# Half differences issued one row half at a time, from two one-bank PSUM tiles

## The chip, the cores and the metric

The kernel runs on one core of a Trainium2 chip. A core has TensorE (PE in the profile; its weight loads are shown as PEld), VectorE (DVE), ScalarE (ACT), GpSimd (POOL) and SyncE (SP), which all take their instructions in order from a queue of their own, and 16 DMA engines. The metric is the time of one execution on the device in microseconds. TensorE writes to PSUM, 8 banks of 512 float32 values for each of 128 partitions; ScalarE and VectorE read it.

## What is computed

Two attentions over the same 2048 tokens, mixed by a gate for each token. Branch A is a sliding, dilated local attention (8 keys a query); branch B is a full attention of 32 heads that share one key and one value head.

```python
def _B_ref(x, wq, wk, wv, wo):
    B, S, D = x.shape
    H = 32; Dh = D // H
    q = (lambda x, *d: x.transpose(*d))((x @ wq).reshape(B, S, H, Dh), 0, 2, 1, 3)
    k = x @ wk
    v = x @ wv
    scores = jnp.einsum("bhqd,bkd->bhqk", q, k) * (Dh ** -0.5)
    p = _softmax(scores, axis=-1)
    o = jnp.einsum("bhqk,bkd->bhqd", p, v)
    return (lambda x, *d: x.transpose(*d))(o, 0, 2, 1, 3).reshape(B, S, H * Dh) @ wo
...
x = A_x
g = _sigmoid((x * gate_w).sum(-1, keepdims=True))
a = _A_ref(x, A_wqkv, A_wo)
b = _B_ref(x, B_wq, B_wk, B_wv, B_wo)
return g * a + (1 - g) * b
```

B = 1, S = 2048, D = 512, head size 16. The change is about the row maxima of branch B's scores, which the softmax subtracts.

## The kernel before

**Units.** Branch B is cut into 32 units: 4 blocks of 512 queries times 8 groups of 4 heads. A unit has 16 exponential steps, one for each block of 128 keys. In a step (exp_pair, weighted) two pairs of matmuls form the scores of 4 heads, keys on the partitions, ScalarE takes the exponential of each pair (2 banks), and four matmuls multiply the result with the values and add into the bank po. The maximum of each query's scores has to be known before its unit starts: it is written into two spare rows of the unit's query tile qst, so that the score matmul subtracts it.

**Maxima.** They come from a second set of score matmuls, queries on the partitions. A slot (v, pr, t, kc) is one unit, one pair of heads, one block of 128 queries and one block of 512 keys; it has two parts, odd = 0 and 1, which lie on the partitions 0 to 63 and 64 to 127 (two row halves of TensorE that can run side by side). The 2048 parts are settled in one of three ways:

- fill_pair: both parts of a slot into the two banks of m2 (pm in the profile), one VectorE reduction of 1024 values (L357).
- fill_one: one part into m1 (ps) or po, one reduction of 512 values (L368). In the exponential steps these are the "singles"; the function singles allows one in a step as long as more parts are left than two a remaining step, and 20 for each output row to come.
- half differences: for two slots with neighbouring key blocks, max(a, b) = (a + b)/2 + |a - b|/2. The keys' half sums and half differences stand in kcd (half_keys, half_parts). fill_diff multiplies the queries with the half differences into m2 (L422), and ScalarE writes the absolute values into a tile dd (L432); fill_sum multiplies with the half sums into m1 or po, and one fused VectorE operation adds |a - b|/2 and takes the maximum (L442), in place in dd. A group is two such slots: two difference matmuls, two absolute values, two sum matmuls, two fused operations, for four parts. In the projections dd is one tile; in an output phase it is two, taken in turn.

**Where half differences run.** In stream, which also issues the projections (queries, then 64 lumps of branch A's projection, 12 matmuls for each row half, 384 wide, two banks eb[0] or eb[1] in turn) and, in out_phase, the output rows (24 matmuls for each half and row, 512 wide). stream walks two positions, at[0] and at[1], one for each row half. In each step it gives each half its next matmul, or a single part in its stead (single, odd); only the other half advances then. After the step it may issue fill_diff, both halves at once, or fill_pair. A lump is emptied by two ScalarE copies (a_post, L251 and L252).

**Order.** All queues are written out in program order by a planner in the kernel: clk holds its clocks for PE, ACT and DVE, free the times at which banks come free, ready_d those of the absolute values; T_R, T_LAT, T_TTR and the like are its costs in microseconds, and after(engine, ready, duration) moves a clock on. pend holds the groups' parts that wait for their sum; slots are taken in order. fill_diff is called if no single part is open (half), pend is empty, and m2 is planned free within 0.1 us and VectorE within 1.3 us. fill_sum is called if its bank is at most 0.1 us and its absolute value at most 0.4 us from free. Output phases start at a unit's first step, when their units are done and the lead (parts settled, in units, less the unit reached) is below LEAD, 3.0; the last four output rows are spread over the last steps, when at most 9 parts are left (L1170).

The tiles m2, m1 and po come from one PSUM pool (pp). m2 serves as the bank of the last lump, of one pair of exponentials after an output phase (exp_pair with other), and of the last output rows too.

Of the kernel before, what the change touches and what calls it, by code (L numbers as in the profile page):

```python
# [6 lines left out]
F32 = mybir.dt.float32  # L7
# [6 lines left out]
P = 128  # L14
# [26 lines left out]
NH = NJ // 2  # L41
TO_END = 10
LEAD, M2S, M1S, E1S, PER_ROW = 3.0, 0.5, 0.3, 0.2, 20


T_R, T_LAT, T_EXP, T_RED2, T_RED1, T_W, T_TTR = 0.23, 0.20, 0.92, 1.14, 0.61, 1.21, 0.66


@with_exitstack
def gated_mix_kernel(ctx, tc, xt, wa, wk, wq, wo_a, wo_b, out):  # L50
# [24 lines left out]


    eb = [pp.tile([P, 2, 512], F32, name=f"pe{k}") for k in range(2)]
    m2 = pp.tile([P, 2, 512], F32, name="pm")
    m1 = pp.tile([P, 512], F32, name="ps")
    po = pp.tile([P, 512], F32, name="po")  # L80

    def split(hi, lo, src, eng=None):
        nc.scalar.activation(hi, src, AF.Copy)
# [266 lines left out]
        tasks.append((after("dve", 0, 0.34) + (2.0 if kcd and not pe else 0.1), shift_a, (v, mt)))  # L350

    def fill_pair(dst, key):
        v, pr, t, kc = slots.pop(0)
        m = unit_tile(v)
        for odd in range(2):
            max_mm(dst[:, odd, :], v, pr, t, kc, odd)
        nc.vector.tensor_reduce(m[:, :, pr, t, kc], dst, AX.X, ALU.max)  # L357
        free[key] = after("dve", after("pe", 0, T_R) + T_LAT, T_RED2) + 0.08
        filled(v, 2)
# [11 lines left out]


    sel, kcd, dd, pend, ready_d, formed, ended, wants = [], [], [], [], [0.0, 0.0], set(), set(), []
    hb = [(m2[:, 0, :], m2[:, 1, :]), (m1, po)]

    def half_sel():

# [10 lines left out]

    def half_keys(g):

        keys = ("m2", "m2") if g == 0 else ("m1", "po")
        clk["pe"] = max(clk["pe"], *(free[k] for k in keys))
        for x in range(2):
            for y in range(2):
                nc.tensor.matmul(hb[g][x], sel[0][:, x * y], kst[:, (2 * g + y) * 512:(2 * g + y + 1) * 512], start=(y == 0), stop=(y == 1))
        clk["pe"] += 1.2
        for k in keys:
            free[k] = clk["pe"] + 4.0
        tasks.append((clk["pe"] + 1.0, half_parts, (g, keys)))
# [20 lines left out]
    def half_mm(dst, v, pr, t, kc, x, odd):  # L420
        b = 64 * odd
        nc.tensor.matmul(dst, qst[home(v)[0]][b:b + 62, pr, t * P:(t + 1) * P], kcd[0][b:b + 62, kc // 2, x, :], start=True, stop=True)  # L422

    def fill_diff():
        v, pr, t, kc = slots.pop(0)
        slots.pop(0)
        for odd in range(2):
            half_mm(m2[:, odd, :], v, pr, t, kc, 1, odd)
        at = after("pe", 0, T_R) + T_LAT
        dd.append(dd.pop(0))  # L430
        for odd in range(2):
            nc.scalar.activation(dd[0][:, odd], m2[:, odd, :], AF.Abs)  # L432
            ready_d[odd] = after("act", at, 0.52) + 0.1
        free["m2"] = ready_d[1]
        pend.extend([(v, pr, t, kc, 0), (v, pr, t, kc, 1)])

    def fill_sum():
        v, pr, t, kc, odd = pend.pop(0)
        m = unit_tile(v)
        dst, key = ((m1, "m1"), (po, "po"))[odd]  # L440
        half_mm(dst, v, pr, t, kc, 0, odd)
        nc.vector.tensor_tensor_reduce(dd[0][:, odd], dst, dd[0][:, odd], 1.0, -FMAX, ALU.add, ALU.max, m[:, odd, pr, t, kc:kc + 1])  # L442
        free[key] = after("dve", max(clk["pe"] + T_R + T_LAT, ready_d[odd]), T_TTR) + 0.08
        filled(v, 2)

# [34 lines left out]
    pe, pexp, exped = [], {}, {}  # L480

    def exp_pair(s, pr, other=False, first=0):
        bank, key = (m2, "m2") if other else (eb[pr], f"e{pr}")
        u, kt = divmod(s, NJ)
        for odd in (first, 1 - first):
            b = 64 * odd
            nc.tensor.matmul(bank[:, odd, :], kst[b:b + 64, kt * P:(kt + 1) * P], qst[home(u)[0]][b:b + 64, pr, :], start=True, stop=True)  # L487
        e = px.tile([P, 2, 512], F32, name="pexp", bufs=6)
        nc.scalar.activation(e, bank, AF.Exp, scale=SCALE)  # L489
        free[key] = after("act", after("pe", free[key], T_R) + T_LAT, T_EXP)  # L490
        exped[s] = free[key]
        pexp[s, pr] = e
# [239 lines left out]
    def stream(seq, mm, done, pooled):  # L732

        at, told = [0, 0], 0
        ended.clear()
        while min(at) < len(seq):
            single, odd = None, -1
            if wants and all(free[k] <= clk["pe"] + 0.1 for k in (("m1", "po") if wants[0] else ("m2",))):
                half_keys(wants.pop(0))
            if pend:  # L740
                if free[("m1", "po")[pend[0][4]]] <= clk["pe"] + 0.1 and ready_d[pend[0][4]] <= clk["pe"] + 0.4:
                    single, odd = fill_sum, pend[0][4]
            elif paired() and not half or 1 in wants:
                pass
            elif fillable() and free["m1"] <= clk["pe"] + 0.1:
                single, odd = lambda: fill_one(m1, "m1"), half[0][4] if half else 0
            elif pooled and fillable() and free["po"] <= clk["pe"] + 0.1:
                single, odd = lambda: fill_one(po, "po"), half[0][4] if half else 0
            dur = 0.0
            for b in (0, 1) if odd != 1 else (1, 0):  # L750
                if b == odd:
                    now = clk["pe"]
                    single()
                    clk["pe"] = now
                elif at[b] < len(seq):
                    dur = mm(b, seq[at[b]])
                    at[b] += 1
            after("pe", 0, dur or T_R)
            if ended or 0 in wants:
                pass  # L760
            elif paired():
                if not half and not pend and max(free["m2"], clk["dve"] - 1.2) <= clk["pe"] + 0.1:
                    fill_diff()
            elif slots and fillable() and free["m2"] <= clk["pe"] + 0.1:
                clk["pe"] = max(clk["pe"], free["m2"])
                fill_pair(m2, "m2")
            while told < min(at):
                told += 1
                done(seq[told - 1])

    def out_phase(js, n, whole_unit):

        m = 3 * (C + n)
        items = {}

        def mm(b, at):
            x, j, i = at
            if j not in items:
                items[j] = out_items(j, n)
                clk["pe"] = max(clk["pe"], free[f"e{x % 2}"])  # L780
            st, mv = items[j][i]
            h = slice(64 * b, 64 * b + 64)
            nc.tensor.matmul(eb[x % 2][:, b, :], st()[h], mv[h], start=(i == 0), stop=(i == m - 1))  # L783
            return T_R

        def done(at):
            x, j, i = at
            if i % 4 == 3:
                run_tasks()
                run_pool()  # L790
            if x == len(js) - 1 and i == m - 5:
                ended.add(1)
            if x == 0 and i == 1:
                turn(j, 1)
            if x == 0 and i == 6:
                later.pop(j)()
            if i == 3 * n and j != js[-1]:
                prepare(js[x + 1], n)
            if i == m - 5 and j != js[-1]:
                turn(js[x + 1], 1 - x % 2)  # L800
            if i == m - 1:
                out_store(j, x % 2)
                if j != js[-1]:
                    later.pop(js[x + 1])()

        if whole_unit:
            formed.update((0, 1))
            free["po"] = max(free["po"], clk["dve"] + 0.1)
            dd[:] = [px.tile([P, 2, 512], F32, name="pexp", bufs=6) for _ in range(2)]
        stream([(x, j, i) for x, j in enumerate(js) for i in range(m)], mm, done, False)  # L810
        while pend:
            odd = pend[0][4]
            clk["pe"] = max(clk["pe"], free[("m1", "po")[odd]], ready_d[odd] - 0.3)
            fill_sum()
            clk["pe"] += T_R
        settle("sum", 0)
        formed.clear()
# [418 lines left out]
    for x in range(2):  # L1236
        for k, w in ((0, woh), (0, wol), (1, woh)):
            for t in range(2):
                nc.tensor.matmul(ends[2 * x + t], tls[x][:, k, t * P:(t + 1) * P], w[1][:, C - 1, :], start=(w is woh and k == 0 and x + t < 2), stop=(k == 1))
        for t in range(2):  # L1240
            j = NJ - 4 + 2 * x + t
            os = px.tile([P, D], F32, name="osl", tag="pexp", bufs=6)
            nc.vector.tensor_add(os, ends[2 * x + t], parts[j])
            (nc.sync, nc.scalar)[t].dma_start(out[0].rearrange("(p j) d -> p j d", j=NJ)[:, j, :], os)
    pe[0].release()
    p2[0].release()
    p2b[0].release()
# [26 lines left out]
```

## Time and profile before

| | us |
|---|---|
| median of 3 runs (1475.98 to 1476.28) | 1476.24 |
| the profiled execution | 1475.43 |
| its span | 1473.6 |
| first and last start of an absolute value in the projections | 101.9, 264.5 |
| the same in the output phases | 847.4, 1220.6 |

The times up to some 100 us are loads, keys, queries and first maxima; to some 266 us branch A's projections with half differences; then the exponential steps to the end, with output phases of 8 rows at about 846 us and of 4 rows at about 1186 us. A row of a group reads: line, engine, operation, output<-input, shapes and count | busy us, mean ns of one | idle time of the engine before it and what ended it. A row by stretch reads: start:end, length, busy us of each engine with its count of instructions, granted clock, DMA share, GB/s. A wait reads: who <- for whom: us in total, times, longest.

### The profile page before, as it was taken

How to read it: one execution, taken by the hardware profiler on the slowest of the kernel's cores; microseconds unless marked ns; L12 is line 12 of the kernel's file. 1: busy time of each engine (PE TensorE's matmuls, PEld its weight loads, DVE VectorE, ACT ScalarE, POOL GpSimd, SP SyncE). 2: the span in 40 equal slices, each digit the busy share in tenths (PEclk: the TensorE clock that was granted, in tenths of full speed). 3: DMA queues.
4: the chain of work that ended last, by engine and by line, in shares of the span. 5: the costliest groups of instructions: out<-in, count | busy, mean ns of one | idle time of the engine just before them, and what ended most of it. 6: DMA issues, size and time to landing. Idle time of an engine off the chain costs nothing.

```text
span 1473.6 us, 29548 instructions
## 1 busy us (share of the span) xinstructions
PE 1461.7 (99%) x10996; PEld 708.0 (48%) x10996; DVE 1193.9 (81%) x1855; ACT 1274.5 (86%) x1646; POOL 1032.6 (70%) x1828
## 2 busy tenths in 40 slices
PE   9999999999999999999999999999999999999998
PEld 5999889533333333333333376333333364333333
DVE  6976667789888888888898878899888878889712
ACT  5468988899999999999999978999999988999986
POOL 7876988887888979888889898888888330111220
PEclk9999999999999999999999999999999999999999
DMA  6754323121220211202112121120120000000110
GB/s 224 209 151 136 93 88 120 34 85 42 66 80 7 85 60 42 71 12 71 45 38 77 36 64 67 42 71 26 57 71 12 12 27 16 13 1 2 29 31 30
DMA packets 54080, 89.86 MB, mean 61 GB/s; under 512 B 18800, under 2 KB 35232, under 8 KB 49712
## 3 DMA queue, kind: packets, MB, share of 16 engines
q1 hardware_dynamic: 46928, 48.99, 11.4%
q0 software_dynamic: 6432, 37.94, 7.8%
q8 instruction: 86, 1.41, 0.4%
q10 hardware_dynamic: 576, 1.05, 0.2%
q14 instruction: 58, 0.48, 0.1%
HBM read 60.07 MB, written 27.35 MB: 59 GB/s over the span
## 4 chain that ended last, share of the span: by engine, by line
PE 91%; ACT 3%; POOL 3%; issue 1%; DVE 1%; DMA 1%; DVEq 0%; POOLq 0%; ACTq 0%
PE po L497 35%; PE pe L487 23%; PE pm L330 8%; PE ps L330 7%; PE pe L1098 7%; PE pe L783 4%; PE pm L422 2%; PE ps L422 1%; PE pm L851 1%; ACT dd L432 1%; PE po L422 1%; POOL qlo L222 1%; POOL qraw L215 1%; PE pe L185 1%; DMA xraw<-xt 1%
## 5 line engine op out<-in xcount | busy, mean ns | idle before, releaser
L489 ACT ACTIVATE pexp<-pe 128x1024 f32<-128x1024 f32 x1022 | 989.5, 1022 | 93.0 <-PE pe L487 90.8
L357 DVE TENSOR_REDUCE mx<-pm 128x2 f32<-128x1024 f32 x495 | 605.8, 1224 | 117.6 <-PE pm L330 113.8
L497 PE MATMUL po<-pexp,vst 128*32 128x512 f32 x4096 | 545.7, 605 | 0.0
L487 PE MATMUL pe<-qst,kst 64*128 64x512 f32 x1916 | 434.5, 447 | 0.4 <-ACT pexp L489 0.3
L487 PEld LDWEIGHTS pe<-qst,kst 64*128 64x128 f32 x1916 | 179.7, 183 | 473.7 <-ACT pexp L489 467.8
L368 DVE TENSOR_REDUCE mx<-ps 128x1 f32<-128x512 f32 x481 | 327.1, 680 | 3.7 <-PE ps L330 3.7
L330 PE MATMUL pm<-kst,qst 62*128 62x512 f32 x945 | 192.0, 396 | 0.3 <-DVE mx L357 0.3
L561 POOL TENSOR_TENSOR pr<-aext 128x256 f32<-128x256 f32 x256 | 182.5, 738 | 2.2 <-DMA aext<-ad 1.9
L330 PE MATMUL ps<-kst,qst 62*128 62x512 f32 x455 | 180.0, 396 | 0.2 <-DVE mx L442 0.2
L621 POOL TENSOR_TENSOR oa<-oa,av 128x256 f32<-128x256 f32 x224 | 164.1, 732 | 15.1
L497 PEld LDWEIGHTS po<-pexp,vst 128*32 128x32 f32 x4096 | 80.8, 108 | 178.2 <-issue 169.1
L618 POOL TENSOR_TENSOR av<-aext,lg 128x256 f32<-128x256 f32 x224 | 139.3, 622 | 12.7
L1098 PE MATMUL pe<-wah,xh 64*128 64x384 f32 (+1 forms) x504 | 109.8, 338 | 0.4 <-ACT gate L255 0.4
L1098 PE MATMUL pe<-wal,xh 64*128 64x384 f32 (+1 forms) x504 | 110.1, 337 | 0.0
L1098 PE MATMUL pe<-wah,xl 64*128 64x384 f32 (+1 forms) x504 | 109.9, 337 | 0.0
L432 ACT ACTIVATE dd<-pm 128x512 f32<-128x512 f32 x164 | 91.0, 608 | 17.8 <-PE pm L422 11.3
L442 DVE CUSTOM_DVE_ANT_0 dd<-ps,dd 128x512 f32<-128x512 f32 x82 | 56.7, 692 | 55.1 <-PE ps L422 28.9
L330 PEld LDWEIGHTS pm<-kst,qst 62*128 62x128 f32 x945 | 92.0, 187 | 2.8 <-DVE mx L357 1.0
L330 PEld LDWEIGHTS ps<-kst,qst 62*128 62x128 f32 x455 | 85.0, 187 | 5.5 <-DVE mx L368 1.7
L567 POOL TENSOR_TENSOR tr<-pr 128x512 f32<-128x512 f32 x64 | 81.7, 1277 | 4.1
L567 POOL TENSOR_TENSOR tr<-tr 128x256 f32<-128x256 f32 (+1 forms) x128 | 72.4, 566 | 8.3
L524 POOL TENSOR_TENSOR rl<-rl,gate_t 128x16 f32<-128x16 f32 x31 | 6.8, 220 | 100.4 <-DVE rl L518 99.9
(215 smaller groups left out, 1896.2 us busy)
## 6 DMA issues: line engine op xcount, KB each, us to landing
aext<-ad POOLq DMA_DIRECT2D x32, 1056.0 KB, 5.5
ad<-stage SPq DMA_DIRECT2D x32, 384.0 KB
qst<-qd SPq DMA_DIRECT2D x60, 128.0 KB
xraw<-xt SPq DMA_DIRECT2D x16, 256.0 KB
qd<-qhi SPq DMA_DIRECT2D x16, 256.0 KB
qd<-qlo SPq DMA_DIRECT2D x16, 256.0 KB
qst<-qd SPq DMA_DIRECT2D x60, 64.0 KB
qst<-ml SPq DMA_DIRECT2D x216, 2.0 KB
```

The source lines that it names most:

```text
L330: nc.tensor.matmul(dst, qst[home(v)[0]][b:b + 62, pr, t * P:(t + 1) * P], kst[b:b + 62, kc * 512:(kc + 1) * 512], start=True, stop=True)
L357: nc.vector.tensor_reduce(m[:, :, pr, t, kc], dst, AX.X, ALU.max)
L368: nc.vector.tensor_reduce(m[:, odd, pr, t, kc:kc + 1], dst, AX.X, ALU.max)
L432: nc.scalar.activation(dd[0][:, odd], m2[:, odd, :], AF.Abs)
L487: nc.tensor.matmul(bank[:, odd, :], kst[b:b + 64, kt * P:(kt + 1) * P], qst[home(u)[0]][b:b + 64, pr, :], start=True, stop=True)
L489: nc.scalar.activation(e, bank, AF.Exp, scale=SCALE)
L497: nc.tensor.matmul(po[32 * i:32 * i + 32, :], vst[:, kt, :], pexp[s, i // 2][:, i % 2, :], start=(kt == 0), stop=(kt == NJ - 1))
L561: nc.gpsimd.tensor_mul(pr[:, k], q, e[:, o:o + NH, AC:2 * AC])
L567: nc.gpsimd.tensor_add(nx, cur[:, :, 0:n], cur[:, :, n:2 * n])
L618: nc.gpsimd.tensor_mul(av, e[:, o:o + NH, 2 * AC:].rearrange("p j (h d) -> p j h d", d=DH), lg[:, w].unsqueeze(3).to_broadcast([P, NH, AG, ...
L621: nc.gpsimd.tensor_add(ao, ao, av)
L1098: nc.tensor.matmul(front[2 if x == last else x % 2][0][:, b, :n], l[h], r[h], start=(i == 0), stop=(i == 3 * C - 1))
```

## The change

A class Banks holds m2, either as one tile of two banks or as two tiles of one bank each; shape(n) releases the one form and takes the other. fill_pair, exp_pair with other, and the whole method ask for one tile; fill_diff and half_keys(0) ask for two. fill_diff now issues the difference matmul and the absolute value of one row half (odd), first 0, then 1; open_group holds the slot between the two. diff_half says whether one may go: no part of the same half in pend, its own bank planned free (half_free), VectorE's clock at most 1.6 us ahead. stream collects up to one part for each row half (lone) and issues these in place of that half's next matmul. pend carries the dd tile of its group. After the stream an open group is finished.

```diff
+M2H = 0.0
...
+class Banks:
...
+    def __init__(self, tc, name):
+        self.tc, self.name, self.pool, self.tiles = tc, name, None, ()
+        self.whole()
+
+    def shape(self, n):
+        if len(self.tiles) != n:
+            if self.pool:
+                self.pool.release()
+            self.pool = self.tc.alloc_tile_pool(name=self.name + "s", bufs=1, space=PSUM)
+            if n == 1:
+                self.tiles = [self.pool.tile([P, 2, 512], F32, name=self.name)]
+            else:
+                self.tiles = [self.pool.tile([P, 512], F32, name=self.name, tag=f"{self.name}{b}") for b in range(2)]
+        return self
+
+    def whole(self):
+        return self.shape(1).tiles[0]
+
+    def __getitem__(self, at):
+        if len(self.tiles) == 1:
+            return self.tiles[0][at]
+        return self.tiles[at[1]][:, at[2]]
...
-    m2 = pp.tile([P, 2, 512], F32, name="pm")
...
+    m2 = Banks(tc, "pm")
...
     def fill_pair(dst, key):
+        if dst is m2:
+            dst = m2.whole()
...
-    hb = [(m2[:, 0, :], m2[:, 1, :]), (m1, po)]
+    hb = {1: (m1, po)}
...
+        if g == 0:
+            hb[g] = (m2.shape(2)[:, 0, :], m2[:, 1, :])
...
+    open_group, half_free = [], [0.0, 0.0]
+
+    def diff_half():
+
+        if max(half_free) != free["m2"]:
+            half_free[:] = [free["m2"]] * 2
+        odd = len(open_group) and 1
+        if any(x[4] == odd for x in pend) or half_free[odd] > clk["pe"] - M2H or clk["dve"] - 1.6 > clk["pe"]:
+            return None
+        return odd
+
     def fill_diff():
-        v, pr, t, kc = slots.pop(0)
-        slots.pop(0)
-        for odd in range(2):
-            half_mm(m2[:, odd, :], v, pr, t, kc, 1, odd)
-        at = after("pe", 0, T_R) + T_LAT
-        dd.append(dd.pop(0))
-        for odd in range(2):
-            nc.scalar.activation(dd[0][:, odd], m2[:, odd, :], AF.Abs)
-            ready_d[odd] = after("act", at, 0.52) + 0.1
-        free["m2"] = ready_d[1]
-        pend.extend([(v, pr, t, kc, 0), (v, pr, t, kc, 1)])
+        if not open_group:
+            open_group.append(slots.pop(0))
+            slots.pop(0)
+            dd.append(dd.pop(0))
+            odd = 0
+        else:
+            odd = 1
+        v, pr, t, kc = open_group[0]
+        m2.shape(2)
+        half_mm(m2[:, odd, :], v, pr, t, kc, 1, odd)
+        nc.scalar.activation(dd[0][:, odd], m2[:, odd, :], AF.Abs)
+        half_free[odd] = ready_d[odd] = after("act", clk["pe"] + T_R + T_LAT, 0.54) + 0.1
+        free["m2"] = max(half_free)
+        pend.append((v, pr, t, kc, odd, dd[0]))
+        if odd:
+            open_group.clear()
 
     def fill_sum():
-        v, pr, t, kc, odd = pend.pop(0)
+        v, pr, t, kc, odd, d = pend.pop(0)
         m = unit_tile(v)
         dst, key = ((m1, "m1"), (po, "po"))[odd]
         half_mm(dst, v, pr, t, kc, 0, odd)
-        nc.vector.tensor_tensor_reduce(dd[0][:, odd], dst, dd[0][:, odd], 1.0, -FMAX, ALU.add, ALU.max, m[:, odd, pr, t, kc:kc + 1])
+        nc.vector.tensor_tensor_reduce(d[:, odd], dst, d[:, odd], 1.0, -FMAX, ALU.add, ALU.max, m[:, odd, pr, t, kc:kc + 1])
         free[key] = after("dve", max(clk["pe"] + T_R + T_LAT, ready_d[odd]), T_TTR) + 0.08
         filled(v, 2)
...
+        bank, key = (m2.whole(), "m2") if other else (eb[pr], f"e{pr}")
...
-            single, odd = None, -1
+            lone = {}
             if wants and all(free[k] <= clk["pe"] + 0.1 for k in (("m1", "po") if wants[0] else ("m2",))):
                 half_keys(wants.pop(0))
             if pend:
                 if free[("m1", "po")[pend[0][4]]] <= clk["pe"] + 0.1 and ready_d[pend[0][4]] <= clk["pe"] + 0.4:
-                    single, odd = fill_sum, pend[0][4]
-            elif paired() and not half or 1 in wants:
+                    lone[pend[0][4]] = fill_sum
+            elif open_group or paired() and not half or 1 in wants:
                 pass
             elif fillable() and free["m1"] <= clk["pe"] + 0.1:
-                single, odd = lambda: fill_one(m1, "m1"), half[0][4] if half else 0
+                lone[half[0][4] if half else 0] = lambda: fill_one(m1, "m1")
             elif pooled and fillable() and free["po"] <= clk["pe"] + 0.1:
-                single, odd = lambda: fill_one(po, "po"), half[0][4] if half else 0
+                lone[half[0][4] if half else 0] = lambda: fill_one(po, "po")
+            if open_group or paired() and not (ended or half or 0 in wants):
+                odd = diff_half()
+                if odd is not None and odd not in lone:
+                    lone[odd] = fill_diff
             dur = 0.0
-            for b in (0, 1) if odd != 1 else (1, 0):
-                if b == odd:
+            for b in sorted((0, 1), key=lambda b: b not in lone):
+                if b in lone:
                     now = clk["pe"]
-                    single()
+                    lone[b]()
                     clk["pe"] = now
                 elif at[b] < len(seq):
                     dur = mm(b, seq[at[b]])
                     at[b] += 1
             after("pe", 0, dur or T_R)
-            if ended or 0 in wants:
-                pass
-            elif paired():
-                if not half and not pend and max(free["m2"], clk["dve"] - 1.2) <= clk["pe"] + 0.1:
-                    fill_diff()
-            elif slots and fillable() and free["m2"] <= clk["pe"] + 0.1:
+            if not (ended or 0 in wants or open_group or paired()) and slots and fillable() and free["m2"] <= clk["pe"] + 0.1:
                 clk["pe"] = max(clk["pe"], free["m2"])
                 fill_pair(m2, "m2")
...
         stream([(x, j, i) for x, j in enumerate(js) for i in range(m)], mm, done, False)
+        if open_group:
+            clk["pe"] = max(clk["pe"], half_free[1], free["m2"])
+            fill_diff()
+            clk["pe"] += T_R
```

The other lines of the diff release the tiles at the end.

More of the change, by code (lines that the diff above doesn't have):

```diff
@@ L482, in exp_pair @@
     def exp_pair(s, pr, other=False, first=0):
-        bank, key = (m2, "m2") if other else (eb[pr], f"e{pr}")
+        bank, key = (m2.whole(), "m2") if other else (eb[pr], f"e{pr}")
         u, kt = divmod(s, NJ)
@@ L1244, in gated_mix_kernel @@
             (nc.sync, nc.scalar)[t].dma_start(out[0].rearrange("(p j) d -> p j d", j=NJ)[:, j, :], os)
+    m2.pool.release()
     pe[0].release()
```

## The prediction

> **What bounds the kernel now.** I read the page's busy times and chain first, then the costliest groups, then stretches of time one by one, because the kernel has stages with different limits.
>
> ```profile
> PE 1461.7 (99%) x10996; PEld 708.0 (48%) x10996; DVE 1193.9 (81%) x1855; ACT 1274.5 (86%) x1646; POOL 1032.6 (70%) x1828
> ...
> PE 91%; ACT 3%; POOL 3%; issue 1%; DVE 1%; DMA 1%; DVEq 0%; POOLq 0%; ACTq 0%
> ```
>
> TensorE is busy for 99% of the span and is 91% of the chain: the order on its queue, and what makes that queue wait, set the time. The change touches three stretches, those that hold half differences (L432 and L442). In the busy times by stretch they stand out by their weight loads:
>
> ```profile
> core 0: us, PE busy (x) PEld busy (x) DVE busy (x) ACT busy (x) POOL busy (x), PEclk, DMA share, GB/s
> 100.00:266.00 166.00, 164.87 (x1662) 150.77 (x1660) 110.84 (x343) 142.92 (x334) 136.75 (x224) 1.00 0.35 108
> 846.00:916.00 70.00, 68.80 (x601) 51.23 (x601) 56.77 (x164) 55.75 (x107) 63.54 (x102) 1.00 0.15 48
> 1186.00:1223.00 37.00, 36.22 (x314) 25.93 (x310) 29.60 (x84) 28.90 (x55) 13.52 (x19) 1.00 0.08 27
> ```
>
> Call them the projection stretch and the two output stretches (8 rows, then 4). The granted clock is 1.00 in all. ScalarE idles 23.1, 14.2 and 8.1 us in them, 45.4 us in all. The absolute values are counted by the group of L432, split by the same stretches:
>
> ```profile
> 100.00:266.00 166.00, 90.97 (x164) 1.00 0.35 108
> 846.00:916.00 70.00, 39.30 (x72) 1.00 0.15 48
> 1186.00:1223.00 37.00, 19.65 (x36) 1.00 0.08 27
> ```
>
> The same stretch's groups on ScalarE give the number of projections (a lump in the code) in it, 56:
>
> ```profile
> L251 ACT ACTIVATE stage<-pe 128x384 f32<-128x384 f32 x56 | 27.5, 492 | 5.2 <-PE pe L1098 3.0 <-POOL wal L84 0.8 <-PE po L422 0.4
> ```
>
> A group (one call of fill_diff before) has two of them, so there are 82, 36 and 18 groups, 136 in all; each settles four maxima of 512 scores, at 2 x 90.97/164 = 1.11 us of ScalarE.
>
> Between these stretches the exponential steps run. TensorE alone, two steps of them:
>
> ```profile
> 432.91 1.07 PE L497 MATMUL po<-pexp,vst 128*32 128x512 f32 x8
> ...
> 434.24 0.40 PE L330 MATMUL pm<-kst,qst 62*128 62x512 f32 x2
> 434.48 0.41 PE L487 MATMUL pe<-qst,kst 64*128 64x512 f32 x2
> 434.73 0.40 PE L330 MATMUL ps<-kst,qst 62*128 62x512 f32 x1
> 435.05 1.07 PE L497 MATMUL po<-pexp,vst 128*32 128x512 f32 x8
> ...
> 436.94 1.06 PE L497 MATMUL po<-pexp,vst 128*32 128x512 f32 x8
> ```
>
> A step with a pair of maxima (pm) and a single one (ps) takes 435.05 - 432.91 = 2.14 us; the next, with the pair alone, 1.89 us. So a single costs about 0.24 us. VectorE's reductions of singles, by stretch, say how many there are:
>
> ```profile
> 270.00:846.00 576.00, 177.87 (x262) 1.00 0.17 53
> 916.00:1186.00 270.00, 82.66 (x122) 1.00 0.14 46
> 1223.00:1389.00 166.00, 51.49 (x76) 1.00 0.03 9
> ```
>
> 460 of them, in nearly every step. A maximum that is settled in a stretch with half differences takes a single out of a step: the function singles drops them as soon as two per remaining step suffice. That is where a gain can come from.
>
> **What the change does.** It adds no operation: per group there are still four 512-wide matmuls, two absolute values, two fused sum-and-maximum operations. It moves the two difference matmuls. Before, both row halves are issued together, only when no sum is pending; after, each half goes alone beside the other half's projection matmul, as soon as its own bank is free in the plan, its own sum has been issued and VectorE is planned at most 1.6 us behind. So it changes how many groups the planner fits in, and what TensorE's queue waits for. Here is such a wait, in order of time:
>
> ```profile
> 182.53 0.34 PE L1098 MATMUL pe<-wal,xh 64*128 64x384 f32 x2
> ...
> 182.68 0.08 DVE L442 DVE_READ_ACCUMULATOR2_ANT mx<- 128x1 f32 x1
> ...
> 182.71 0.35 PE L1098 MATMUL pe<-wah,xl 64*128 64x384 f32 x2
> ...
> 182.86 1.15 ACT L432 ACTIVATE dd<-pm 128x512 f32<-128x512 f32 x2
> ...
> 183.59 0.69 DVE L442 CUSTOM_DVE_ANT_0 dd<-ps,dd 128x512 f32<-128x512 f32 x1 [0.22 <-ACT dd L432]
> ...
> 183.90 0.48 ACT L251 ACTIVATE stage<-pe 128x384 f32<-128x384 f32 x1
> 184.06 0.19 PEld L422 LDWEIGHTS pm<-kcd,qst 62*128 62x128 f32 x2 [0.41 <-ACT dd L432]
> 184.06 0.49 PE L422 MATMUL pm<-kcd,qst 62*128 62x512 f32 x2
> ...
> 184.21 0.08 DVE L442 DVE_READ_ACCUMULATOR2_ANT mx<- 128x1 f32 x1
> ...
> 184.27 0.50 ACT L252 ACTIVATE two<-pe 128x384 f32<-128x384 f32 x1
> ...
> 184.39 0.34 PE L1098 MATMUL pe<-wal,xh 64*128 64x384 f32 x2
> ```
>
> The pair of absolute values ends at 184.01; the next pair of differences starts at 184.06, both halves, though the first bank must have been read by about 183.5. One tile for two banks makes half 0 wait for half 1.
>
> *What a group costs TensorE.* Projection pairs follow each other in 182.71 - 182.53 = 0.18 us; in the step above the pair pm at 434.24 gives way to the next matmul at 434.48, 0.24 us. Four half matmuls are two such pairs: 0.46 us (0.23 each) by this stage's rate, before as after. What hides them: nothing, TensorE is the bound. A group is worth four singles at 0.24 us less: 0.96 - 0.46 = 0.50 us net.
>
> *How many groups more.* I stepped both issue rules by hand with the planner's constants (0.18 us a projection step, 0.23 + 0.20 to the absolute value, 0.54 for it, 0.66 for the fused operation, 0.8 for a projection's two copies). The old rule settles at a group per 1.49 us, ScalarE idling some 0.45 us of it, and with the copies at 1.61 groups per projection of 12 steps. The new one starts the next half 0 while half 1 is still read: after a first lump the planned ScalarE has hardly a gap, and three lumps of 2.88 us hold 11 absolute values, 1.83 groups per lump. 82 x 1.83/1.61 = 93; the gates and other small operations take their share from both, so I take 92, 10 more. In an output row (24 steps of 0.23, 2.4 us of copies on ScalarE) the plan holds 4.5 groups at 87% of ScalarE; at the 96% of the new rule 0.96 x (6.0 + 0.46g) = 2.4 + 1.08g gives 5.3. That is 6 and 3 more. Sum: 19. Bounds: 0 (the plan's ScalarE is full already) and 45.4/(1.11 - 0.46) = 70 (ScalarE never idle). I take 19, near the lower end, because the planner's clock counts, not the chip's, and its ScalarE is at 90% already.
>
> *What waits come and go.* Waits of the projection stretch, then of the first output stretch:
>
> ```profile
> DVE dd L442 <- ACT dd L432: 23.2, 27, 3.3
> ACT dd L432 <- PE pm L422: 11.3, 18, 0.9
> PEld pm L422 <- ACT dd L432: 11.3, 39, 0.7
> ...
> ACT dd L432 <- DVE mx L442: 5.9, 8, 0.9
> ```
>
> ```profile
> ACT pexp L432 <- PE pm L422: 12.2, 20, 1.2
> ...
> PEld pe L783 <- ACT turned L679: 4.1, 7, 0.7
> PEld pm L422 <- ACT pexp L432: 2.8, 12, 0.3
> ```
>
> TensorE's wait for the bank, 11.3 + 2.8 us of idle weight load (39 waits of 0.29 us, part of it under a running matmul), is what separate tiles can shorten: the least is 0, a gain of 14 us. Against that stands the buffer dd: the projection stretch has one. The absolute value overwrites what the fused operation of the group before has read (above, 182.68 + 0.08, then 0.10 us to the start at 182.86). From 182.86 over the fused operation at 183.59 and its read-out to 184.29 and 0.10 more is 1.53 us: a half cannot come round faster, while the new plan puts some groups 1.08 us apart. ScalarE then stands in that wait, with the projection's copies (L251, L252) queued behind it, and TensorE follows when its bank is late. By that loop a lump with 1.64 groups takes 1.53 x 1.64 + 0.45 (the two copies take 0.87 us, 183.90 to 184.77 above; 1.53 - 1.11 = 0.42 of it fits into the loop's gap) = 2.96 us against 12 x 0.18 + 0.46 x 1.64 = 2.91 of TensorE: 0.05 us x 56 lumps = 3 us. So the waits are put at +3 us, between -14 and the +14 of the rival below. The output stretches have two dd buffers and are spared this.
>
> The tiles that change shape cost only at a change of stage, where pm is drained before as after; I set them at 0, and at 4 such changes with one 0.41 us wait each it would be 2 us. More maxima done early raise the planner's lead, which can put an output stretch 16 steps later, past some of the loads of queries on SP's queue and of branch A's work on POOL: the same rows, copies and stores, at 0 as long as the last four rows still come after the singles.
>
> *A rule against it.* The Trainium skill (TensorEngine Tiling (Array Packing), Performance Considerations, on the PSUM bottleneck) says that splitting the array into tiles speeds up TensorE but not the emptying of PSUM. The stretch's ScalarE row agrees (142.92 of 166 us); by that rule no group comes on top, which is the second rival below.
>
> **The sum.** 19 groups x 4 x 0.24 = 18.2 us off the steps; 19 x 0.46 = 8.7 on in the stretches; +3 waits: -6.5 us. The profiled execution took 1475.43 us (span 1473.6), so 1468.9; the median of the runs lies 0.8 higher, which gives **1470 us**.
>
> **Rivals.**
>
> *The gaps of ScalarE really fill.* If the earlier issue fills ScalarE two thirds of the way to its bound, 45 groups at 0.50 us: -22 us, 1454. For it: the 12.2 us in which ScalarE waited for pm. Against: the planner issues by its own clock, and that one is nearly full.
>
> *Nothing changes.* ScalarE sets the number of groups, a few come on top and their 0.46 us and the waits eat them: 1473 to 1478. For it: 86% of ScalarE in the stretch, and the read-out loop of 1.53 us; against: 45.4 us of idle ScalarE.
>
> *Two waits where there was one: slower.* TensorE's queue is in order, and each half difference is now an entry of its own that can stand in front of the other half's projection. Before, 39 of 82 pairs waited 0.29 us. If the same share of 184 halves waits as long, that is 88 x 0.29 = 25.4 us against 11.3, +14, and with the late copies behind the dd loop (0.15 us on 92 groups) another +14 at worst. Without the 3 us of above: -9.5 + 14 = +4.5, up to +18; 1481 as its middle (1480 to 1494). It decides from 9.5/184 = 52 ns more wait per half. For it: the plan is fuller and doesn't know of the weight splits (L83) and the dd loop, so it has less room to catch up. Against: each half has its own bank, and the chip's TensorE is slower than planned (166 us against 56 x 12 x 0.18 + 82 x 0.41 = 155 by the constants), which gives ScalarE time.
>
> **Chances.** Forecast 0.52 (its own range 1464 to 1473.2), gaps filled 0.10, nothing 0.15, slower 0.23. Runs of this kernel agree to 0.02%; I count 0.2%, 3 us, as no change. Faster by more: 0.60 (nearly all of the forecast, and the filled gaps); within: 0.16; slower: 0.24. The range reaches over half of each outer case: 1458 to 1485.
>
> **What would show it.** In the projection stretch more than 164 absolute values, some 184, and it ends some 8 us later; some 84 and 42 in the output stretches; some 76 fewer singles on ps in the steps, each such step at 1.90 us. Weight loads of pm wait after one absolute value, not two. Wrong if the number of absolute values stays, if the weight load's wait on pm grows beyond 20 us (rival slower), or if ScalarE's wait for VectorE grows from 5.9 us to above 20 us with the copies late.

## The result: slower, and the profile after

| | before | after |
|---|---|---|
| median of the runs, us | 1476.26 (4 runs) | 1487.92 (4 runs) |
| ratio, 95% interval | | 1.0079 (1.0061 to 1.0096) |
| span of the profiled execution, us | 1473.6 | 1485.9 |
| groups: projections, 8 rows, 4 rows | 82, 36, 18 | 86, 39, 20 |
| first weighted step, us | 269.12 | 282.51 |
| 8 rows with the step around them, us | 71.30 | 73.05 |
| 4 rows with the step around them, us | 37.03 | 38.36 |

The forecast was 1470 us; the kernel became slower, and by more than the range allowed. The last three rows come from the timeline of TensorE: from one run of value matmuls (weighted) to the next. The two that mark the end of the projections, before:

```profile
269.12 1.07 PE L497 MATMUL po<-pexp,vst 128*32 128x512 f32 x8
```

and after:

```profile
282.51 1.06 PE L545 MATMUL po<-pexp,vst 128*32 128x512 f32 x8
```

The 12.3 us of span divide as follows: projections +13.4, output stretches +1.75 and +1.33, exponential steps and what follows them -4.2 (29 singles and 5 pairs fewer in the steps). So nearly all of it is lost in the projections, for four groups more. By stretch, after (engines as in the prediction's table: PE, PEld, DVE, ACT, POOL):

```profile
100.00:279.00 179.00, 177.56 (x1674) 149.50 (x1672) 118.34 (x358) 147.87 (x340) 134.11 (x213) 1.00 0.33 101
854.00:928.00 74.00, 74.00 (x631) 54.20 (x625) 61.95 (x173) 62.61 (x116) 65.76 (x102) 1.00 0.15 50
1199.00:1237.00 38.00, 37.81 (x323) 27.85 (x321) 32.21 (x88) 32.03 (x58) 14.31 (x19) 1.00 0.10 33
```

TensorE seems as full as before, though its matmuls' ends are modelled; the loss shows in the waits. Those of the projections, after (L478 is the absolute value, L490 the fused operation, L454 the matmuls of half differences and half sums):

```profile
ACT dd L478 <- DVE mx L490: 25.8, 39, 1.1
DVE dd L490 <- ACT dd L478: 22.9, 25, 1.4
POOL stage L289 <- ACT two L280: 19.6, 22, 2.4
PEld pm L454 <- ACT dd L478: 19.3, 55, 0.8
...
PEld po L454 <- DVE mx L490: 3.5, 13, 0.3
PEld ps L454 <- DVE mx L490: 3.4, 13, 0.3
```

Before, ScalarE waited for VectorE 5.9 us in 8 waits, now 25.8 us in 39; TensorE's weight loads for pm waited 11.3 us, now 19.3, and ps and po are new: 26.2 us in all against 11.3. The prediction had named this sign, a wait of ScalarE for VectorE above 20 us, as one that would show it wrong. The absolute values as a group, before and after:

```profile
L432 ACT ACTIVATE dd<-pm 128x512 f32<-128x512 f32 x164 | 91.0, 608 | 17.8 <-PE pm L422 11.3
```

```profile
L478 ACT ACTIVATE dd<-pm 128x512 f32<-128x512 f32 x172 | 99.1, 610 | 28.7 <-DVE mx L490 25.8
```

One place where ScalarE waits, in order of time (after):

```profile
201.59 0.39 PE L454 MATMUL pm<-kcd,qst 62*128 62x512 f32 x1
201.72 0.69 DVE L490 CUSTOM_DVE_ANT_0 dd<-ps,dd 128x512 f32<-128x512 f32 x1 [1.03 <-ACT dd L478]
...
202.34 0.08 DVE L490 DVE_READ_ACCUMULATOR2_ANT mx<- 128x1 f32 x1
202.34 0.69 DVE L490 CUSTOM_DVE_ANT_0 dd<-po,dd 128x512 f32<-128x512 f32 x1
...
202.52 0.60 ACT L478 ACTIVATE dd<-pm 128x512 f32<-128x512 f32 x1 [0.81 <-DVE mx L490]
...
203.16 0.18 PEld L454 LDWEIGHTS pm<-kcd,qst 62*128 62x128 f32 x1 [0.39 <-ACT dd L478]
...
203.38 0.50 ACT L280 ACTIVATE two<-pe 128x384 f32<-128x384 f32 x1
...
203.90 0.53 ACT L111 ACTIVATE wah<-waraw 128x384 fp32r<-128x384 f32 x1
...
204.34 1.07 ACT L478 ACTIVATE dd<-pm 128x512 f32<-128x512 f32 x2
...
204.95 0.69 DVE L490 CUSTOM_DVE_ANT_0 dd<-po,dd 128x512 f32<-128x512 f32 x1 [1.10 <-ACT dd L478]
204.97 0.18 PEld L454 LDWEIGHTS pm<-kcd,qst 62*128 62x128 f32 x1 [0.39 <-ACT dd L478]
```

The next group's half difference is in the bank soon after 201.59, ScalarE is free, but it may write dd only when the fused operation of 201.72 has been read out (202.34 + 0.08). It starts at 202.52, 0.81 us idle. Then everything on its queue is late: the weight load at 203.16 waits for the bank it has just emptied, the projection's copy and a weight split come behind it, and at 204.97 the next weight load waits again. One late buffer holds three engines, one after the other. The two halves of dd did not wait for each other here: the fused operation of half 1 (po, at 202.34) ran on to 203.03, across the start of the absolute value of half 0 at 202.52.

### The profile page after: what moved, and what is told of

The parts are those of the page before. It is cut to its first block, busy times and chain, and to the rows that moved or that the text cites. A ratio compares the mean times of both kernels' runs of the same rounds, so it can differ in the third digit from the quotient of the medians.

```text
span 1485.9 us, 29738 instructions
## 1 busy us (share of the span) xinstructions
PE 1474.7 (99%) x10996; PEld 706.9 (48%) x10996; DVE 1186.1 (80%) x1858; ACT 1287.9 (87%) x1664; POOL 1033.7 (70%) x1828
## 3 DMA queue, kind: packets, MB, share of 16 engines
q1 hardware_dynamic: 46928, 48.99, 11.3%
q8 instruction: 86, 1.41, 0.4%
## 4 chain that ended last, share of the span: by engine, by line
PE 93%; POOL 2%; ACT 2%; DVE 1%; issue 1%; DMA 1%; DVEq 0%; POOLq 0%; ACTq 0%
PE po L545 34%; PE pe L535 23%; PE pm L358 8%; PE pe L1149 7%; PE ps L358 7%; PE pe L830 4%; PE pm L454 3%; PE ps L454 2%; PE po L454 2%; PE pm L902 1%; POOL qlo L250 1%; POOL qraw L243 1%; PE pe L213 1%; DMA xraw<-xt 1%; ACT dd L478 1%
## 5 line engine op out<-in xcount | busy, mean ns | idle before, releaser
L398 DVE TENSOR_REDUCE mx<-ps 128x1 f32<-128x512 f32 x447 | 304.6, 681 | 2.9 <-PE ps L358 2.8
L358 PE MATMUL ps<-kst,qst 62*128 62x512 f32 x426 | 168.5, 396 | 0.0
L666 POOL TENSOR_TENSOR av<-aext,lg 128x256 f32<-128x256 f32 x224 | 139.6, 623 | 12.4
L1149 PE MATMUL pe<-wal,xh 64*128 64x384 f32 (+1 forms) x504 | 135.7, 343 | 0.0
L1149 PE MATMUL pe<-wah,xh 64*128 64x384 f32 (+1 forms) x504 | 134.9, 344 | 0.4 <-ACT gate L283 0.4
L1149 PE MATMUL pe<-wah,xl 64*128 64x384 f32 (+1 forms) x504 | 134.5, 343 | 0.0
L478 ACT ACTIVATE dd<-pm 128x512 f32<-128x512 f32 x172 | 99.1, 610 | 28.7 <-DVE mx L490 25.8
L490 DVE CUSTOM_DVE_ANT_0 dd<-ps,dd 128x512 f32<-128x512 f32 x86 | 59.3, 690 | 33.1 <-PE ps L454 16.3
L289 POOL TENSOR_TENSOR stage<-stage,two 128x384 f32<-128x384 f32 x64 | 65.0, 1016 | 28.6 <-ACT two L280 21.0
L490 DVE CUSTOM_DVE_ANT_0 dd<-po,dd 128x512 f32<-128x512 f32 x86 | 59.3, 690 | 27.9 <-PE po L454 13.3
```

The lines of the kernel that those rows point to most:

```text
L398: nc.vector.tensor_reduce(m[:, odd, pr, t, kc:kc + 1], dst, AX.X, ALU.max)
L490: nc.vector.tensor_tensor_reduce(d[:, odd], dst, d[:, odd], 1.0, -FMAX, ALU.add, ALU.max, m[:, odd, pr, t, kc:kc + 1])
L666: nc.gpsimd.tensor_mul(av, e[:, o:o + NH, 2 * AC:].rearrange("p j (h d) -> p j h d", d=DH), lg[:, w].unsqueeze(3).to_broadcast([P, NH, AG, ...
L1149: nc.tensor.matmul(front[2 if x == last else x % 2][0][:, b, :n], l[h], r[h], start=(i == 0), stop=(i == 3 * C - 1))
```

## The experiments

Two theories were put against each other. L: the loop through the single dd buffer holds ScalarE, and with it the rest. Q: each half difference is now an entry of its own in TensorE's queue and stands there, whatever dd does (the prediction's slower rival). The runs were made in several series, and the kernel before was run again in each (1475.39, 1475.82 and 1475.53 us); ratios are to the kernel before of the same series.

**A second dd buffer, in both kernels.** A second dd takes 4 KB more of each partition; the place of unit 7's query tile, which isn't used before the steps begin, serves. Its loads move to the first step.

```diff
-        dd.append(pm[0].tile([P, 2, 512], F32, name="dd", bufs=1))
+        dd.extend([pm[0].tile([P, 2, 512], F32R, name="dd", bufs=1), q67[:, 1]])
...
-            if m > 4 and m % 2 and len(stacked) < NB:
+            if m > 4 and m % 2 and len(stacked) < NB - 1:
...
+            if len(stacked) == NB - 1:
+                clear(NB - 1, nc.gpsimd)
             stack(len(stacked))
```

> The changed kernel with a second dd buffer in the projections (the space of unit 7's query tile, which is loaded only when the steps begin; the absolute values are rounded to fp32r there). Theory L (the loop through the single dd: an absolute value waits for the fused operation that read the buffer, ScalarE stands, its copies and banks are late, TensorE's queue stands): ScalarE's wait for VectorE in the projections falls from 25.8 us to under 6, the first weighted step comes 8 to 12 us sooner than at 282.5 us, time 1476 to 1480. Theory Q (each half difference is an entry of its own in TensorE's queue and may stand there, whatever dd does): 3 us at most, 1485 to 1488.

Measured: 1475.59 us (ratio to the kernel before 0.9999, 0.9990 to 1.0008), 12.3 us below the changed kernel (11.5 when each is taken against the kernel before of its own series), with the same 86 groups in the projections. That is a little more than L expected. The first weighted step:

```profile
269.89 1.07 PE L545 MATMUL po<-pexp,vst 128*32 128x512 f32 x8
```

12.6 us sooner. No wait of ScalarE for VectorE's fused operation is left in the projections. What is left of the waits of TensorE's weight loads in the projections (second buffer):

```profile
PEld ps L454 <- DVE mx L490: 5.4, 15, 2.1
...
PEld pm L454 <- ACT dd L478: 0.9, 4, 0.4
```

The wait for pm is gone (19.3 to 0.9 us), though each half is still an entry of its own. L holds; Q as the main cause falls, though a small share of it isn't excluded.

> The kernel before with the same second dd buffer, as a control. There ScalarE waited for VectorE only 5.9 us. L: at most 3 us off, 1473 to 1476. Q: no difference, 1475 to 1477.

Measured: 1473.99 us (0.9989, 0.9980 to 0.9998), 1.4 us off, as L expected. The buffer is worth little to the old order and some 12 us to the new one.

**One tile of two banks in the changed kernel.**

```diff
     def shape(self, n):
+        n = 1
         if len(self.tiles) != n:
```

> The changed kernel, same order, but m2 is always one tile of two banks. If the split does what it says, the difference of half 0 waits for the absolute value of half 1 again: up to 0.5 us for most of the 145 groups, 1500 to 1530. If the banks of one tile were tracked apart, nothing changes: 1488. L and Q don't differ here.

Measured: 1623.75 us (1.1000, 1.0982 to 1.1018), 136 us more than the changed kernel, where 42 were expected at most. The absolute value, its idle time and for whom, with 140 of the 172 weight loads of pm in the projections (all 172 wait 110.7 us):

```profile
L479 ACT ACTIVATE dd<-pm 128x512 f32<-128x512 f32 x172 | 103.6, 602 | 105.8 <-DVE mx L491 57.5 <-PE pm L455 41.5 <-PE ps L455 2.2
...
L455 PEld LDWEIGHTS pm<-kcd,qst 62*128 62x128 f32 x140 | 26.2, 187 | 92.5 <-ACT dd L479 92.2
```

The projections alone end 90 us later (372.32 against 282.51 us). So the split does what it says, and the new order isn't worth having without it: the two halves of a group are no longer together, and with one tile each half waits for whatever the other one is doing. Not all of the 136 us is waiting: in eight stretches of 3.4 us the granted clock was 0.50, which accounts for 14 us at most, half of their length.

**Two one-bank tiles in the kernel before**, both halves still issued at once (m2.shape(2) in the old fill_diff).

> The kernel before, same order (both halves at once), with m2 as two one-bank tiles for the differences. The first of the two matmuls no longer waits for the second absolute value, but the second one still does and it follows at once. L and Q: 0 to 4 us off, 1472 to 1476; the weight loads' wait for pm (11.3 us in the projections) stays above 6.

Measured: 1472.52 us (0.9982, 0.9972 to 0.9991), 2.9 us off; the weight loads' wait for pm in the projections is 9.9 us. Both are as expected.

**What a single is worth.** The slots of the last key block are left out for units 30 and 31, whose maxima are then taken over three quarters of the keys.

```diff
+    slots = [x for x in slots if x[0] < NU - 2 or x[3] < 3]
     half = []
...
-                left[x] = NF // NU
+                left[x] = NF // NU - (16 if x >= NU - 2 else 0)
```

> The kernel before without 32 of the 2048 maxima parts: units 30 and 31 take theirs from the first three of four key blocks. What is a single worth? By the prediction's row (one step without a single, 1.90 us against 2.14) 32 x 0.24 = 7.7 us off, 1467.7. By the floor that ScalarE's two exponentials set when such steps follow each other (2.01 us a step in the changed kernel from 1328 to 1403 us) 32 x 0.12 = 3.8 us off, 1471.5.

Measured: 1471.93 us against 1475.82 (0.9974, 0.9963 to 0.9985): 3.9 us for 32 parts, 0.12 us each (0.07 to 0.17 by the interval), not 0.24. The trace has 32 single reductions fewer (449 for 481) and as many pairs as before (495), so singles are what was removed. The changed kernel's steps show why they are worth so little. TensorE, three steps in a row without a single:

```profile
1340.78 1.06 PE L545 MATMUL po<-pexp,vst 128*32 128x512 f32 x8
...
1342.83 1.06 PE L545 MATMUL po<-pexp,vst 128*32 128x512 f32 x8
...
1344.79 1.06 PE L545 MATMUL po<-pexp,vst 128*32 128x512 f32 x8
```

and ScalarE there:

```profile
1338.35 3.83 ACT L537 ACTIVATE pexp<-pe 128x1024 f32<-128x1024 f32 x4 [0.20 <-PE pe L535]
1342.37 5.04 ACT L537 ACTIVATE pexp<-pe 128x1024 f32<-128x1024 f32 x5 [0.19 <-PE pe L535]
```

The steps take 2.05 and 1.96 us, 2.01 in the mean of all 37 that follow each other there. The first row's four exponentials, those of two steps, take 3.83 us, and with the wait of 0.19 us before the next row 4.02 us: ScalarE is nearly full, and now and then it waits for the next scores. The step of 1.90 us in the prediction stood alone among steps with a single. It was no accident: the trace of before has 21 such lone steps, nearly all at 1.90 us. But 37 in a row can't go at that rate; a lone one seems to use up a little slack of ScalarE.

**A planner that knows dd**, in the changed kernel.

```diff
-        ... or clk["dve"] - 1.6 > clk["pe"]:
+        ... or clk["dve"] - 1.6 > clk["pe"] or len(dd) == 1 and read_d[odd] - T_R - T_LAT > clk["pe"]:
...
-        ... after("act", clk["pe"] + T_R + T_LAT, 0.54) + 0.1
+        ... after("act", max(clk["pe"] + T_R + T_LAT, read_d[odd] if len(dd) == 1 else 0.0), 0.54) + 0.1
...
+        read_d[odd] = free[key] + 0.1
```

> The changed kernel with a planner that knows the single dd buffer: in the projections a half difference is issued, and its absolute value is planned, only after the planned end of the fused operation that still reads that half of dd. Nothing else changes, TensorE's queue still has each half as an entry of its own. L: the 12 us in the projections come back whole or nearly, with fewer groups there (76 to 84), 1474 to 1478. Q: the halves still stand in the queue, 1482 or more.

Measured: 1478.42 us (1.0018, 1.0009 to 1.0027), just above the range. It planned 69 groups, fewer than expected. The profiled execution is the longest of the ten (1481.26 us). The absolute values and the first weighted step:

```profile
L478 ACT ACTIVATE dd<-pm x138: 570/618/662, 101.9 to 252.1; 128x512 f32<-128x512 f32 x138
```

```profile
256.83 1.07 PE L546 MATMUL po<-pexp,vst 128*32 128x512 f32 x8
```

and the waits of the projections:

```profile
ACT dd L478 <- PE pm L454: 9.5, 19, 0.7
...
PEld pm L454 <- ACT dd L478: 3.5, 3, 3.1
...
ACT dd L478 <- DVE mx L490: 0.7, 2, 0.3
```

The stall is gone without a second buffer: 25.7 us sooner for 17 groups less, of which 17 x 0.46 = 7.8 us are the groups. But the maxima come short later, and the steps, nearly all with a single already, can't take them up: one step with a pause to catch up takes 5.26 us. TensorE in it, and a row by stretch (PE, PEld, DVE, ACT, POOL) for the time behind it:

```profile
817.23 0.40 PE L358 MATMUL ps<-kst,qst 62*128 62x512 f32 x1
819.16 0.80 PE L536 MATMUL pe<-qst,kst 64*128 64x512 f32 x2 [1.52 <-DVE mx L387]
819.88 1.94 PE L546 MATMUL po<-pexp,vst 128*32 128x512 f32 x8
```

```profile
819.00:826.00 7.00, 6.84 (x30) 2.21 (x31) 2.39 (x6) 3.16 (x4) 4.98 (x13) 0.52 0.33 113
```

The granted clock is 0.52 in the mean of these 7 us, and the two steps behind the pause take 3.44 and 3.23 us. So part of this run's later loss is the clock of the execution that was profiled, and the plan's missing groups can't be priced from it.

**The allowance alone**, 0.8 us of planned VectorE work where the change has 1.6, with one buffer and with two.

```diff
-        ... clk["dve"] - 1.6 > clk["pe"]:
+        ... clk["dve"] - 0.8 > clk["pe"]:
```

> The changed kernel, one dd buffer in the projections, but a half difference goes only when VectorE is planned at most 0.8 us behind (1.6 in the change). The absolute value starts 0.43 us after the issue at the earliest, so it can stand for VectorE some 0.4 us at most instead of 1.2. L: ScalarE's wait for VectorE in the projections falls from 25.8 us to under 12, and the time to 1476 to 1482. If the allowance doesn't matter: 1486 to 1489.

Measured: 1482.42 us (1.0054, 1.0037 to 1.0070), 0.4 us above the range that L expected; ScalarE's wait for VectorE is 19.5 us, not under 12. The smaller allowance goes the right way, but doesn't stand for the missing condition.

> The same allowance of 0.8 us in the kernel with the second dd buffer. With the same buffers and two one-bank tiles the old order took 1469.9 and the new one 1475.6. If the rest of the difference is TensorE's queue standing at the sum matmuls until VectorE has emptied ps and po (19.4 us of idle weight load there), that wait falls below 10 us and the time to 1470 to 1473. If it is the halves standing as entries of their own (Q), it stays at 1474 to 1477.

Measured: 1473.88 us (0.9989, 0.9980 to 0.9998), between the two expectations. Idle weight loads for ps and po, over the whole run, are down from 19.4 to 7.6 us, as expected, and the time only by 1.7. All of that lies before the first weighted step (268.21 against 269.89 us), 0.46 of it for one group less. The output stretches hold 17 groups fewer (45 for 62), and yet the time from the first weighted step to the last hardly moves, 1192.33 against 1192.07 us.

**The new rule in the output stretches only**; the projections keep one tile of two banks and the old fill_diff (in the lines not shown).

```diff
-            if open_group or paired() and not (ended or half or 0 in wants):
+            if not pooled and (open_group or paired() and not (ended or half or 0 in wants)):
```

> The changed rule only in the two output stretches, which have two dd buffers; the projections keep both halves at once, one tile of two banks and the old rule. L: the projections end as before (269 us), and the rest is worth what it was in the changed kernel, 1 us less than before (1190.97 against 1192.01 us from the first weighted step to the last): 1474 to 1476. Q: the output stretches get longer by more than 3 us each, 1478 or more.

Measured: 1476.02 us (1.0002, 0.9992 to 1.0011): no difference. The 1 us less that L expected didn't come (1192.44 us from the first weighted step to the last), nor did Q's 3 us a stretch. There are 40 and 20 groups, 4 and 2 more, and the stretches take 72.85 and 37.88 us, 1.55 and 0.85 more. In these stretches, where dd has two buffers, the change neither gains nor loses.

**Both buffers for the old order**, from the two controls.

> The kernel before, both halves at once, with two one-bank tiles for the differences and the second dd buffer: the two controls put together. If their gains (2.9 and 1.4 us) come from separate waits they add up, 1471; if from the same wait, 1472.5.

Measured: 1469.89 us (0.9958, 0.9946 to 0.9971), faster than both kernels. 2.9 and 1.4 us make 4.3, and 5.9 came. In times of runs that difference isn't clear of the intervals; in the profiled executions the first weighted step shows it: 0.97 us sooner with the two tiles (268.15), 0.44 with the second buffer (268.68), and together 4.89:

```profile
264.23 1.06 PE L530 MATMUL po<-pexp,vst 128*32 128x512 f32 x8
```

The waits fit: the weight loads for pm waited 11.3 us before, 9.9 with the tiles, 10.6 with the buffer and 4.1 with both. Each seems to have been held still by the wait that the other one removes.

## Why the prediction was wrong, point by point

- **TensorE's order sets the time: right.** The loss goes with time in which its queue stands: the weight loads' waits for pm, ps and po in the projections, 26.2 us against 11.3.
- **A group costs 0.46 us: right in size.** In the output stretches of the last but one experiment 6 groups came for 2.4 us, 0.40 each. In the changed kernel itself 5 came for 3.1 us, 0.62 each, so some waits came with them.
- **A single is worth 0.24 us: wrong, the step failed.** It is 0.12 us (3.9 us for 32 parts). With it a group is worth 4 x 0.12 - 0.46 = 0.02 us: nothing. The forecast of a gain was wrong here, before any wait. The run with 17 groups fewer in its output stretches and 0.26 us more from the first weighted step to the last agrees. The row of 1.90 us was a step by itself, while the steps that the change frees follow each other, 37 in a row at the end of the maxima. The trace of before has a few such steps in a row there, and they alternate (2.13, 1.90, 2.12 us):

```profile
1382.64 1.07 PE L497 MATMUL po<-pexp,vst 128*32 128x512 f32 x8
...
1384.77 1.07 PE L497 MATMUL po<-pexp,vst 128*32 128x512 f32 x8
...
1386.67 1.06 PE L497 MATMUL po<-pexp,vst 128*32 128x512 f32 x8
...
1388.79 1.07 PE L497 MATMUL po<-pexp,vst 128*32 128x512 f32 x8
```

- **19 groups more: too many, 9 came** (4, 3, 2 for 10, 6, 3). For the output rows the sum itself was off: 24 steps of 0.23 us are 5.5 us, not the 6.0 that it uses, and with 5.5 it gives 4.5 groups, none more than before. That 3 and 2 came there is luck as far as this sum goes. Why the plan had room for only four more in the projections wasn't taken apart. The rule of the Trainium skill that the prediction weighed (TensorEngine Tiling (Array Packing), Performance Considerations) says that splitting the array doesn't speed up the emptying of PSUM. The traces agree: an absolute value took 608 ns before and 610 ns after. What the prediction drew from it, no group on top, didn't come.
- **The dd loop at 3 us: the mechanism was right, the size wrong.** The projections became 13.4 us longer, 4 x 0.46 = 1.8 of it for groups, so 11.6 us are waits; the second buffer took 12.6 back. The step that failed is the mean over a lump, 2.96 against 2.91 us: it lets a short round be made good by a long one. The loop is 1.53 us in the prediction's row and 1.41 at its shortest in the trace after. By the planner's own clocks (worked out from the kernel's code, not from a run) 29 of the 85 rounds from one group to the next are shorter than that, 1.12 to 1.3 us, and the others 1.6 us and more; before, none was under 1.47. What these 29 lack of the loop adds up to 5.7 us at 1.41 and 9.2 at 1.53, an estimate of the same order as the 11.6 us. With the second buffer, where nothing holds them, rounds down to 1.20 us stand in the trace. That TensorE's queue, once late, doesn't catch up in the longer rounds is our reading; no run shows it by itself.
- **The slower rival** had the sign, and its side clause (the late copies behind the dd loop, up to 14 us) nearly the size. Its mechanism wasn't the one: with a second buffer 172 entries still stand alone in the queue and their weight loads wait 0.9 us for pm, where the rival had 25.4.
- **Waits for one bank in place of two: right.** In the old order the split was worth 2.9 us, well under the 14 us of its bound.

So the sum, in the prediction's terms: the steps gave 4.2 us and not 18.2, nine groups cost some 4.1 and not 8.7, and the waits cost some 12.4 (11.6 in the projections, the rest in the output stretches) and not 3. That makes the 12.3 us of span. Two terms failed, the price of a single and the waits of the dd loop; the first took the gain away, the second made the loss.

What stays open: with the same tiles and buffers the new order takes 1475.59 us and the old one 1469.89. 5.7 us lie before the first weighted step (269.89 against 264.23), 1.8 of it for four more groups. Of the other 3.8 us the waits for ps and po are a candidate: there are none in the old order's projections, 8.5 us in the new one's. With the smaller allowance they are down to 1.5 us, and the projections still end 4.0 us later than the old order's (268.21 against 264.23), 1.4 of it for three groups. The rest was not settled, and a small part of theory Q may be in it. The ten runs of the new order with two buffers also spread over 3.6 us (1473.70 to 1477.32), the five of the old one over 0.7.

## What to carry to other kernels

When a schedule is made tighter, look for the buffer that the old slack had hidden: here a condition that the planner lacks cost little until two uses came closer than the loop through that buffer. Price a step that is saved by several of them in a row, where the next engine's limit shows, not by one that stands alone. And a PSUM tile of several banks was one thing to wait for here: split it where its parts are used at different times.

## What was not expected of the hardware

Two waits seem to have hidden each other: at the end of the projections the one-bank tiles gave 0.97 us, the second buffer 0.44, both 4.89. And one order of instructions, with a dependence across two banks put back, went from 1487.9 to 1623.8 us: in the projections ScalarE idled 105.8 us before the absolute values and TensorE's weight loads 110.7 us for them.

The clock came in unasked. With the planner that knows dd, TensorE stood for 1.52 us up to 819.16 us, and the granted clock was 0.50 from 818.9 to 825.7 us; it stood for 1.80 us up to 1425.74 us, and the clock was 0.50 from 1426.5 to 1429.9. A stand of 2.72 us at 138 us in the same trace left it at 1.00. What decides isn't shown by these runs.
